# FFT convolution on Trainium2: blocks of 4 channels with both parts of the spectrum, in place of blocks of 8 channels of one part

## The chip, the core and the metric

The kernel runs on one core of one Trainium2 chip. A core has five engines with instruction streams of their own: TensorE (PE in the profile; its weight loads stand apart as PEld), VectorE (DVE), ScalarE (ACT), GpSimd (POOL) and SyncE (SP), which here does nothing but issue DMAs. They work on an on-chip memory of 128 partitions; TensorE writes to a second one, PSUM, from which VectorE and ScalarE copy. The metric is the device time of one launch in microseconds (us).

## The reference, cut to what matters

The input is a sequence of 2048 rows of 512 channels in bf16. Two kinds of layer alternate, each on a layer norm of its input, each added to it:

```python
x = A_u
x = x + _A_ref(_layernorm(x), ...)     # long convolution
x = x + _B_ref(_layernorm(x), ...)     # local attention: 32 heads, 8 keys at distances 0, 2, ..., 14
x = x + _A_ref(_layernorm(x), ...)     # the same convolution, same parameters
x = x + _B_ref(_layernorm(x), ...)

def _A_ref(u, A_re, A_im, B_re, B_im, C_re, C_im, log_dt, Dskip):
    ...
    P = jnp.exp(logdA[:, :, None] * l[None, None, :])
    K = jnp.einsum("dn,dnl,dn->dl", Cc, P, dB).real        # a kernel of 2048 taps for each channel
    L2 = 2 * L
    Kp = jnp.pad(K, ((0, 0), (0, L)))
    ...
    Kf = rfft2(Kp[:, None, :])
    Uf = rfft2(up[:, :, None, :])
    Yf = Uf * Kf[None, :, :, :]
    y = irfft2(Yf, (1, L2))[:, :, 0, :L]
    return y + u * Dskip
```

What the change touches is the convolution: the spectrum of the input times the kernel's spectrum, a complex product for each channel and frequency, and the way back. Both convolution layers have the same kernel, so its spectra are worked out in the first and kept in device memory for the second.

## The kernel before, in words

**Stages.** The program runs a short preparation, the first convolution together with the making of the kernel spectra (`kernel_and_first_conv`, to about 206 us), the first attention layer (`b_layer`), the second convolution (`a_layer`, about 323 to 377 us) and the second attention layer. X, the running sum, stays on chip throughout.

**The transform.** A row index is 16p + j, with p over the 128 partitions and j from 0 to 15. The transform of a channel is made in two stages.
- First stage (L840 in the first convolution, L1119 in the second): for each j, two matmuls (real and imaginary part) of 128 channels, into `ps_s`. Copies take it to `Z` (L845, L1123), which holds [128 frequencies k1, 16 groups of 8 channels, 2 parts, 16 j x 8 channels].
- Turn: a block is 4 groups, that is 32 channels with both parts, 128 x 1024 values in 8 squares of 128 x 128. It is transposed into `zt` either by one DMA on SP's queue (L854, L1134) or by 8 matmuls against the identity and a copy (`pt`, L871 and L1140, copies at L1144). Each square holds one part of 8 channels, so that its 128 partitions are 16 j x 8 channels. There are four blocks for each of four groups of 128 channels.
- Second stage (`mm2` L860 to L863, `s2` L1158 to L1161): 4 matmuls of 512 columns against the constants `C2` (cosine, sine and minus sine, each spread over 8 channels by a Kronecker product): real part from real and imaginary, imaginary part from both. The result `xp` is copied to `sp_u` or `xc` for the input (L867, L1165) and to `sp_k` for the kernel.

**The product.** Spectrum x = (xr, xi) times kernel k = (kr, ki). Two products of 1024 on VectorE (L931 and L932, L1176 and L1177): pa = (xr kr, xi kr), pb = (xr ki, xi ki), the kernel part repeated over both halves. Then, in some blocks, two half-sized additions on VectorE (the join: L936 and L937, L1181 and L1182) make the complex product, and the inverse's second stage takes 8 matmuls of 256 columns against `IC`; in the other blocks there is no join, and the inverse takes 16 such matmuls, which add the four partial products in PSUM (L951 to L955, L1196 to L1200). Which blocks are joined is part of the written order.

**The way back.** `vp` is copied to `VT` in two halves (L959, L1205); when the four blocks of a channel group are done, `final` multiplies by `F1T`, adds X with a matmul against the identity (`ps_y`, L978 and L981, L1219 and L1222), and a copy writes X (L985, L1227).

**The kernel spectra.** In the first convolution tables of exponentials are built on VectorE (`Ttab`, `Y2tab`, L391 and L456; some sums go through TensorE instead, `ps_sum` L431 and L432, with a copy on ScalarE, L436), contracted on TensorE (`psk` L469 and L472), stored and fetched again in another layout (`k_scratch`), and transformed as above. Each block of `sp_k` is stored to `kt_scratch` (L922, 256 KB, 16 in all). The second convolution loads it into `Kt` (L1235, one DMA of 256 KB for a block, four tiles of four blocks), issued on SP's queue as soon as the space that `Kt` takes is free; it lies over tiles of the first attention layer.

**The order of the work.** Nothing is scheduled at run time or by the compiler. Five lists of numbers (`ORDERS`), one for each stage, say in which order the operations are issued; the operations are registered with `pl.op`, and where there are alternatives (`pl.either`: a turn by DMA or TensorE, a copy on ScalarE or VectorE, a join or none, a sum on VectorE or on TensorE and ScalarE) the list holds the one that is taken. Each engine issues its own part of the list in that order and waits, at each instruction, for what it needs. Tiles come from pools of a fixed number of buffers (`sp_k` 4, `sp_u` 8, `zt` 4 and 6, `xc` 4, `pa` and `pb` 2 and 3).

Two places that the steps of the prediction rest on:

```python
nc.vector.tensor_tensor(pa[:], x[:], k[:, 0:1, :].to_broadcast([128, 2, 512]), ALU.mult)
nc.vector.tensor_tensor(pb[:], x[:], k[:, 1:2, :].to_broadcast([128, 2, 512]), ALU.mult)
...
Kl[dc, c] = pl.op("S", 0.35, lambda dc=dc, c=c: nc.sync.dma_start(Kt[dc][:, c], kt_dram[dc, :, c]), lag=2.0)
```

Of the kernel before, what the change touches and what calls it, by code (L numbers as in the profile page):

```python
# [11 lines left out]
ALU = mybir.AluOpType  # L12
# [32 lines left out]
STASH = ()  # L45


# [3 lines left out]
def _fft_consts():  # L51
# [10 lines left out]
    cr = np.cos(a16)  # L62
    ci = -np.sin(a16)
    I8 = np.eye(8)

    def kron_jk(m):
        return np.einsum('jk,de->jdke', m, I8).reshape(128, 128)
    C2 = np.stack([kron_jk(cr), kron_jk(ci), kron_jk(-ci)], axis=1)
    crp = np.cos(a16).T
    cip = np.sin(a16).T  # L70

    def kron_kj(m):
        return np.einsum('kj,de->kdje', m, I8).reshape(128, 128)
    CR, CI = kron_kj(crp), kron_kj(cip)
    IC = np.stack([np.concatenate([CR, CI], axis=1), np.concatenate([-CR, -CI], axis=1),
                   np.concatenate([-CI, CR], axis=1)], axis=1)
# [46 lines left out]
def load_b_weights(nc, const, wqkv, wo):  # L123
# [9 lines left out]
    VX = const.tile([128, 2, NV + NJ, 256], BF, name="VX")  # L133
    nc.gpsimd.memset(VX[0:1, :, 0:NV], 0.0)
    return dict(wqk=wqk, wv=wv, wo=wo_t), VX

# [59 lines left out]
def load_params(nc, pp, prm):  # L196
# [16 lines left out]
    "1 2 5 3 7 8 9 10 24 25 11 229 12 15 13 29 30 14 33 26 34 21 27 20 233 44 50 41 297 46 51 47 22 61 58 56 68 23 59 "  # L213
    "60 37 69 74 72 237 42 86 75 235 48 87 38 88 100 231 90 298 299 300 245 91 303 77 76 239 253 101 104 108 249 225 "
    "241 106 93 304 107 115 307 92 136 120 247 122 251 109 227 255 123 137 114 308 152 156 154 243 158 320 321 155 258 "
    "159 256 259 257 125 166 164 260 174 261 168 167 311 301 175 322 302 185 323 190 169 262 191 312 324 263 180 270 "
    "305 184 182 325 306 183 264 268 266 206 326 196 317 198 131 139 200 207 309 138 292 201 327 294 290 199 219 288 "
    "146 310 213 212 218 328 124 280 276 313 314 315 141 147 130 286 282 284 316 272 140 278 274 318 296 319",
    "39 3 37 40 6 38 41 7 47 50 9 4 51 52 10 53 12 42 0 56 13 15 54 16 57 58 59 60 17 25 19 168 18 26 49 22 30 102 48 "
    "88 31 169 170 89 23 103 108 90 111 91 94 105 109 92 62 32 171 106 112 172 95 173 174 134 96 97 98 175 178 33 63 "  # L220
    "27 64 180 100 65 123 181 182 28 183 66 67 68 190 126 69 128 135 71 127 118 72 184 113 188 186 189 136 191 138 187 "
    "131 139 132 142 192 137 269 73 270 271 272 143 140 141 121 275 74 159 79 145 122 276 277 146 278 147 273 81 148 "
    "133 279 116 149 82 155 156 83 84 162 283 163 281 244 117 86 157 245 246 284 85 247 87 289 193 248 194 34 195 292 "
    "290 196 158 152 197 286 199 249 206 200 201 202 153 293 203 349 250 205 208 287 251 214 309 254 350 315 258 210 "
    "351 222 352 212 295 259 256 257 296 216 224 220 353 299 166 304 228 218 260 264 316 354 267 355 312 266 265 226 "
    "262 313 263 317 321 357 268 318 358 359 164 307 323 374 322 375 319 230 376 308 167 324 297 377 302 380 381 382 "
    "320 378 383 314 360 365 303 384 298 429 430 232 340 372 234 236 386 369 343 431 326 370 327 335 330 367 368 344 "
# [253 lines left out]
def prepare(nc, pp, pst, raw, identf, block, ones, M, cb, T, ln, X):  # L481
# [215 lines left out]
    pl.run()  # L697


def kernel_and_first_conv(nc, tc, C, prm, x2d, const, kt_dram, kscr, udram, eps):  # L700
    with ExitStack() as es:
        mt = es.enter_context(tc.tile_pool(name="k_mt", bufs=1))
        M = Multipliers(mt, const)
# [205 lines left out]
        def k_fft(dc):  # L909
# [8 lines left out]
            for c in range(n // 32):  # L918
                keep(dc, c)
# [810 lines left out]
```

## Time and profile before

| what | us |
|---|---|
| median of 3 runs | 496.88 |
| the 3 runs | 496.77, 496.88, 498.36 |
| span of the profiled execution (its own time), first to last instruction | 495.2 |

The median of the runs is 1.7 above the span of the profiled execution.

Busy time by stage, from the profile's view of stretches:

| stage | length | PE | VectorE | ScalarE | DMA share |
|---|---|---|---|---|---|
| preparation and first convolution, 0 to 206 | 206.0 | 145.3 | 195.7 | 172.3 | 0.54 |
| first attention layer, 206 to 322.8 | 116.8 | 108.0 | 106.1 | 72.1 | 0.30 |
| second convolution, 322.8 to 377.3 | 54.5 | 50.5 | 50.7 | 49.2 | 0.56 |
| second attention layer, 377.3 to 495.2 | 117.9 | 107.6 | 105.2 | 55.5 | 0.29 |

How to read the lines that follow. A group line names a line of the kernel, the engine, the operation, the tile written <- the tiles read, the shapes, and the number of instructions; after the bar stand the busy time in us and the mean length of one in ns, and after the second bar the idle time of that engine just before these instructions, and what ended it. A line of the timeline has the start, the length, and the instructions run together in it. A line of the stretches has the stretch, its length, and then the busy time of PE, PEld, VectorE, ScalarE and GpSimd, with the number of instructions, the granted clock of TensorE (1.00 is full), the share of time for which the DMA engines were busy, and GB/s. For SP, whose work is to issue DMAs, the same place holds its busy time alone. Successive instructions of an engine overlap by a little, so that the distance from start to start is shorter than the length.

### The profile page before, as it was taken

How to read it: one execution, taken by the hardware profiler on the slowest of the kernel's cores; microseconds unless marked ns; L12 is line 12 of the kernel's file. 1: busy time of each engine (PE TensorE's matmuls, PEld its weight loads, DVE VectorE, ACT ScalarE, POOL GpSimd, SP SyncE). 2: the span in 40 equal slices, each digit the busy share in tenths (PEclk: the TensorE clock that was granted, in tenths of full speed). 3: DMA queues.
4: the chain of work that ended last, by engine and by line, in shares of the span. 5: the costliest groups of instructions: out<-in, count | busy, mean ns of one | idle time of the engine just before them, and what ended most of it. 6: DMA issues, size and time to landing. Idle time of an engine off the chain costs nothing.

```text
span 495.2 us, 12551 instructions
## 1 busy us (share of the span) xinstructions
PE 411.3 (83%) x5262; PEld 244.4 (49%) x5279; DVE 457.7 (92%) x774; ACT 349.0 (70%) x522; POOL 13.0 (3%) x63
## 2 busy tenths in 40 slices
PE   2602397988898989789999889979998999997996
PEld 1501262665575667543355434565675434563343
DVE  6999999999999998859899999988999689999996
ACT  6999986988778769764664359878997657643340
POOL 0000000000000004000000000000000000000000
PEclk9999698999999999999999989989999999999999
DMA  8930025448556846280031232559901500222217
GB/s 263 197 160 0 1 68 130 81 115 192 114 114 162 152 109 195 68 126 32 18 91 38 58 65 42 165 125 210 182 4 21 112 29 31 77 61 58 42 29 205
DMA packets 101596, 48.81 MB, mean 99 GB/s; under 512 B 86443, under 2 KB 93868, under 8 KB 101284
## 3 DMA queue, kind: packets, MB, share of 16 engines
q1 hardware_dynamic: 101108, 47.62, 41.6%
q8 instruction: 41, 0.67, 0.6%
q10 hardware_dynamic: 432, 0.39, 0.2%
q14 instruction: 15, 0.12, 0.1%
HBM read 15.78 MB, written 8.13 MB: 48 GB/s over the span
## 4 chain that ended last, share of the span: by engine, by line
PE 35%; DVE 12%; DMA 8%; ACT 7%; issue 5%; SPq 1%; POOL 0%; DVEq 0%; ACTq 0%
PE ps_qk L1324 7%; PE po L1503 4%; DVE prod L1487 4%; PE ps_v L1344 4%; PE ps_o L1560 3%; DVE prod L1375 3%; DMA VX<-VX 2%; PE Lp L1385 2%; DMA zt<-Z 2%; PE ps_y L1222 1%; PE vp L1196 1%; PE vp L1200 1%; DMA xnT<-xn 1%; ACT L L1474 1%; ACT Z L845 1%
## 5 line engine op out<-in xcount | busy, mean ns | idle before, releaser
L1375 DVE TENSOR_TENSOR prod<-qT,kT 128x2048 bf16<-128x2048 bf16 (+1 forms) x80 | 76.9, 1006 | 12.6 <-ACT kT L1329 9.9
L1487 DVE TENSOR_TENSOR prod<-VX,L 128x2048 bf16<-128x2048 bf16 (+2 forms) x96 | 77.3, 862 | 1.3 <-DMA VX<-VX 1.0
L1324 PE MATMUL ps_qk<-xnT,wqk 128*128 128x512 bf16 x256 | 61.4, 380 | 1.5 <-DMA xnT<-xn 1.3
L1503 PE MATMUL po<-prod,sb_ident 128*128 128x512 bf16 x216 | 53.5, 379 | 4.8 <-DVE prod L1487 3.7
L1324 PEld LDWEIGHTS <-wqk 128*128 128x128 bf16 x256 | 22.8, 97 | 31.9 <-issue 9.7
L1503 PEld LDWEIGHTS <-sb_ident 128*128 128x128 bf16 x224 | 21.2, 98 | 31.3 <-DVE prod L1487 5.1
L1344 PE MATMUL ps_v<-wv,xnT 128*128 128x256 bf16 x256 | 32.1, 273 | 1.9 <-ACT xnT L1302 1.4
L431 PE MATMUL ps_sum<-Ttab,sb_ident 128*128 128x512 bf16 x36 | 15.1, 420 | 22.2 <-DVE Ttab L391 21.4
L1349 ACT CAST VX<-ps_v 128x512 bf16<-128x512 f32 x32 | 18.6, 587 | 19.8 <-PE ps_v L1344 19.7
L845 ACT CAST Z<-ps_s 128x1024 bf16<-128x1024 f32 (+1 forms) x32 | 29.4, 983 | 3.4 <-PE ps_s L840 2.4
L1560 PE MATMUL ps_o<-wo_t,oT 128*128 128x512 bf16 x108 | 29.4, 388 | 0.6 <-DVE X L1543 0.2
L1329 ACT CAST qT<-ps_qk 128x512 bf16<-128x512 f32 x31 | 17.9, 587 | 16.8 <-PE ps_qk L1324 16.7
L1344 PEld LDWEIGHTS <-xnT 128*128 128x128 bf16 x256 | 24.1, 98 | 10.0 <-issue 3.4
L1523 ACT CAST ot<-po 128x1024 bf16<-128x1024 f32 x14 | 13.8, 1014 | 21.4 <-PE po L1503 21.4
L1385 PE MATMUL Lp<-prod,sb_bones 128*32 128x512 bf16 x256 | 25.6, 390 | 3.6 <-DVE prod L1375 3.6
L456 DVE TENSOR_TENSOR Ttab<-Ttab,MPA 128x2048 bf16<-128x2048 bf16 (+2 forms) x20 | 28.4, 1434 | 0.1
L456 DVE TENSOR_TENSOR Y2tab<-Ttab,MPB 128x6144 bf16<-128x6144 bf16 (+1 forms) x13 | 27.3, 2123 | 0.6 <-PE psk L472 0.6
L1329 ACT CAST kT<-ps_qk 128x512 bf16<-128x512 f32 x32 | 18.7, 586 | 10.9 <-PE ps_qk L1324 10.7
L840 PEld LDWEIGHTS <-sb_F 128*128 128x128 bf16 x256 | 16.1, 103 | 18.3 <-issue 15.7
L153 DVE BATCH_NORM_STATS2 ln_st_b<-X 128x6 f32<-128x128 bf16 (+2 forms) x80 | 23.0, 358 | 0.3 <-ACT X L985 0.3
L436 ACT CAST Ttab<-ps_sum 128x1024 bf16<-128x1024 f32 (+1 forms) x20 | 18.3, 940 | 6.0 <-PE ps_sum L432 4.6
L469 PE MATMUL psk<-Ttab 128*32 128x64 bf16 x1024 | 21.5, 199 | 1.1 <-DVE Ttab L456 0.9
(228 smaller groups left out, 1035.2 us busy)
## 6 DMA issues: line engine op xcount, KB each, us to landing
X<-in_A_u_dram SPq DMA_DIRECT2D x8, 512.0 KB, 5.4
kt_scratch<-sp_k SPq DMA_DIRECT2D x16, 256.0 KB, 3.3
Kt<-kt_scratch SPq DMA_DIRECT2D x16, 256.0 KB, 5.0
k_scratch<-KTq SPq DMA_DIRECT2D x7, 256.0 KB, 2.6
KT<-k_scratch SPq DMA_DIRECT2D x7, 256.0 KB, 3.7
VX<-VX SPq DMA_DIRECT2D x4, 448.0 KB, 4.4
kT<-kT SPq DMA_DIRECT2D x8, 192.0 KB, 2.2
out_dram<-X SPq DMA_DIRECT2D x3, 512.0 KB, 3.6
```

The lines of the kernel that those rows point to most:

```text
L153: self.nc.vector.bn_stats(self.st[:, j, part, :], X[:, j, a:b])
L456: nc.vector.tensor_tensor(d, src.to_broadcast([128, c, n, 2 * EYB]), mm.to_broadcast([128, c * n, EYB, 2]), ALU.mult)
L469: nc.tensor.matmul(o.rearrange("e (s i) -> e s i", s=2), xs, T[:, 1:3, h, m // 2, :, t], start=(m == 0), stop=False, skip_group_check=True)
L845: nc.scalar.copy(box["Z", kind, dc][:, 0:n // 8, :, jq * 32:(jq + 1) * 32].rearrange("p g r k -> p r g k"), box.pop(("s1", kind, dc, jq))[ ...
L1324: nc.tensor.matmul(ps[:], wqk[:, ct, f0:f0 + 128], xnT[:, 4 * s:4 * s + 4, ct, :], start=(ct == 0), stop=(ct == 3))
L1329: copy((qT, kT)[which][fp][:, f2, o:o + 512], box.pop(("qk", which, fp, f2, s))[:])
L1344: nc.tensor.matmul(ps[:, jj].rearrange("p t h d -> p (t h d)"), xnT[:, j + jj, ct, :], wv[:, ct, fp * 256:(fp + 1) * 256], start=(ct == 0) ...
L1375: nc.vector.tensor_tensor(pr[:, 0:n2], qT[fp][:, a:a + n2, j0 * 128:j0 * 128 + 1024], kT[fp][:, a:a + n2, c0:c0 + 1024], ALU.mult)
L1385: nc.tensor.matmul(Lp[r0:r0 + 32, w // 4, :], bones[:, w % 4, :], pr[:, f2 - a, hb * 512:(hb + 1) * 512], start=(n == 1), stop=(n == 4), s ...
L1487: nc.vector.tensor_tensor(p2[:, 0:nj].rearrange("p j t d h -> p (j t) d h"), VX[:, fp, NV + a:NV + a + nj].rearrange("p j (t d h) -> p (j ...
L1503: nc.tensor.matmul(po[:, c:c + 512], ident[:], p2[:, k + j:k + j + 2].rearrange("p j t d h -> p (j t d h)"), start=(n == 1), stop=(n == W))
L1560: nc.tensor.matmul(ps, box["oT"][:, ft // 2, j, ft % 2, :], wo_t[:, ft, :], start=(ft == 0 and not res), stop=(ft == 3))
```

## The change

A block is now 8 groups of 4 channels, and a square of 128 x 128 holds both parts of 4 channels: 2 parts x 16 j x 4 channels on its partitions once it is turned. `Z` is [128, 32, 2, 64].
- The second stage multiplies by one constant of 128 x 128 that takes both parts to both parts: 2 matmuls of 512 columns for a block. Partitions 0 to 63 of the result are the real parts, 64 to 127 the imaginary parts.
- The kernel spectrum is held as [128, 2, 1024]: once as it is, and once with the two halves of the partitions swapped. In the first convolution the swapped copy is made either by two DMAs of 64 partitions on SP's queue (`trade`) or by two more matmuls against a constant with swapped columns and a copy (`again`). The new lists take `trade` for 15 of the 16 blocks. Only the unswapped copy is stored (256 KB as before), and the second convolution loads each block by three DMAs: the whole, and the two halves to the other half's partitions. `Kt` is now 16 tiles of 512 KB.
- The product is one instruction of 2048 for a block, the input's spectrum repeated: (xr, xi) times (kr, ki), and (xr, xi) times (ki, kr). There is no join.
- The inverse's second stage takes 16 matmuls of 128 columns for a block; the signs lie in `IC`.
- `sp_k` has 3 buffers (before 4), `sp_u` 7 (8). A route by which spectra of the input could be parked in device memory, which was not in use, is removed. VX, a tile of the attention layer, is taken and zeroed in each attention layer, before once for both.
- All five lists of the order are new, the attention layers' too, and in them some copies, sums and turns go another way than before (a copy on VectorE for one on ScalarE, and the like).

The core of the diff (the lists, the removed route and repeated passages left out):

```diff
-    C2 = np.stack([kron_jk(cr), kron_jk(ci), kron_jk(-ci)], axis=1)
...
+    I4 = np.eye(4)
+
+    def rows(m):
+        return np.einsum('rjsk,de->rjdske', m, I4).reshape(128, 2, 64)
+    fwd = np.stack([np.stack([cr, ci], axis=1), np.stack([-ci, cr], axis=1)], axis=0)
+    C2 = rows(fwd)
+    C2 = np.stack([C2.reshape(128, 128), C2[:, ::-1].reshape(128, 128)], axis=1)
+    c, z = np.cos(a16).T, np.sin(a16).T
+    re, im = np.stack([c, z], axis=1), np.stack([-z, c], axis=1)
+    IC = np.stack([rows(np.stack([re, -re], axis=0)).reshape(128, 128), rows(np.stack([im, im], axis=0)).reshape(128, 128)], axis=1)
...
-                    xp = box["xp", kind, dc, i] = psA.tile([128, 2, 512], F32, name="xp", tag="psA")
-                    nc.tensor.matmul(xp[:, 0, :], C2[:, 0, :], z[:, :, 0, :], start=True, stop=False)
-                    nc.tensor.matmul(xp[:, 0, :], C2[:, 2, :], z[:, :, 1, :], start=False, stop=True)
-                    nc.tensor.matmul(xp[:, 1, :], C2[:, 1, :], z[:, :, 0, :], start=True, stop=False)
-                    nc.tensor.matmul(xp[:, 1, :], C2[:, 0, :], z[:, :, 1, :], start=False, stop=True)
...
+        def second(kind, dc, i, after, copies):
+            z, swap = ("zt", kind, dc, i), ("swap", dc, i)
+
+            def mm(k):
+                zt = box.pop(z) if k or kind == "u" or (swap, 0) in pl.taken else box[z]
+                xp = box["xp", kind, dc, i, k] = psA.tile([128, 1024], F32, name="xp", tag="psA")
+                for h in range(2):
+                    nc.tensor.matmul(xp[:, h * 512:h * 512 + 512], C2[:, k, :], zt[:, h * 4:h * 4 + 4, :], start=True, stop=True)
...
+            def trade():
+                x = box[kind, dc, i]
+                nc.sync.dma_start(x[0:64, 1, :], x[64:128, 0, :])
+                nc.sync.dma_start(x[64:128, 1, :], x[0:64, 0, :])
...
+                Pd["ks", dc, i] = pl.either(swap, lambda: pl.op("S", 0.9, trade, a, lag=2.4), lambda: again("A", 0.92, nc.scalar.copy),
+                                            lambda: again("V", 1.14, nc.vector.tensor_copy))
+                Sd["k", dc, i] = pl.op("S", 0.35, lambda: nc.sync.dma_start(kt_dram[dc, :, i], box["k", dc, i][:, 0, :]), a,
+                                       drop=("kt", dc, i), lag=3.0)
...
-                nc.vector.tensor_tensor(pa[:], x[:], k[:, 0:1, :].to_broadcast([128, 2, 512]), ALU.mult)
-                nc.vector.tensor_tensor(pb[:], x[:], k[:, 1:2, :].to_broadcast([128, 2, 512]), ALU.mult)
...
-                nc.vector.tensor_tensor(pa[:, 0, :], pa[:, 0, :], pb[:, 1, :], ALU.subtract)
-                nc.vector.tensor_tensor(pa[:, 1, :], pa[:, 1, :], pb[:, 0, :], ALU.add)
...
+                pp = box["pa", dc, c] = wk.tile([128, 2, 1024], BF, name="pa", tag="pa")
+                nc.vector.tensor_tensor(pp[:], x[:].unsqueeze(1).to_broadcast([128, 2, 1024]), k[:], ALU.mult)
...
+                for g in range(8):
+                    for k in range(2):
+                        nc.tensor.matmul(vp[:, g // 4, :, g % 4, :], pp[:, k, g * 128:(g + 1) * 128], IC[:, k, :],
+                                         start=(k == 0), stop=(k == 1))
...
-                Kl[dc, c] = pl.op("S", 0.35, lambda dc=dc, c=c: nc.sync.dma_start(Kt[dc][:, c], kt_dram[dc, :, c]), lag=2.0)
+                def load(dc=dc, c=c):
+                    t = Kt[dc][c]
+                    nc.sync.dma_start(t[:, 0, :], kt_dram[dc, :, c])
+                    nc.sync.dma_start(t[0:64, 1, :], kt_dram[dc, 64:128, c])
+                    nc.sync.dma_start(t[64:128, 1, :], kt_dram[dc, 0:64, c])
+                Kl[dc, c] = pl.op("S", 1.2, load, lag=3.0)
```

## The prediction

> **What bounds the kernel now.** I read the per-core view first (one core, mean granted clock 0.979, so no throttle to explain), then busy time by stretches, then the chain that ended last, then the groups of the lines that change, then the timeline of the DMA queue.
>
> ```profile
> core 0: us, PE busy (x) PEld busy (x) DVE busy (x) ACT busy (x) POOL busy (x), PEclk, DMA share, GB/s
> 70.00:110.00 40.00, 33.67 (x889) 20.32 (x887) 39.38 (x47) 32.64 (x39) 0.71 (x6) 0.96 0.46 101
> 110.00:150.00 40.00, 36.37 (x770) 24.79 (x768) 39.76 (x49) 32.50 (x42) 0.47 (x4) 1.00 0.70 148
> 150.00:200.00 50.00, 44.69 (x933) 32.54 (x932) 47.33 (x81) 40.44 (x58) 6.06 (x1) 1.00 0.66 158
> ...
> 335.00:345.00 10.00, 9.68 (x73) 6.05 (x73) 8.76 (x18) 9.72 (x13) 0.00 (x0) 1.00 1.03 215
> 345.00:355.00 10.00, 9.68 (x83) 6.74 (x83) 9.61 (x20) 8.50 (x14) 0.00 (x0) 1.00 0.94 188
> 355.00:365.00 10.00, 10.00 (x85) 7.14 (x84) 9.83 (x20) 10.00 (x19) 0.00 (x0) 1.00 0.38 76
> ```
>
> Two stages are touched. In the first (tables, kernel spectra and first convolution, up to about 206 us) VectorE is busy for 98 to 99% from 70 to 150 us: the bound is VectorE's sum of work. In the second convolution layer (first matmul at 322.85, last copy of X from 376.70) TensorE, VectorE and ScalarE are all near full, and up to 355 the DMA engines are too.
>
> ```profile
> PE 35%; DVE 12%; DMA 8%; ACT 7%; issue 5%; SPq 1%; POOL 0%; DVEq 0%; ACTq 0%
> ```
>
> The chain changes engine all the time; no single wait carries the end. So I sum the work of each engine by stage, and then look for new waits.
>
> ```profile
> L1176 DVE TENSOR_TENSOR pa<-xc,Kt 128x1024 bf16<-128x1024 bf16 x16 | 11.0, 686 | 0.7 <-ACT xc L1165 0.5 <-ACT X L1227 0.2
> L1181 DVE TENSOR_TENSOR pa<-pa,pb 128x512 bf16<-128x512 bf16 x15 | 6.3, 420 | 0.2
> L936 DVE TENSOR_TENSOR pa<-pa,pb 128x512 bf16<-128x512 bf16 x6 | 2.5, 420 | 0.1
> L1375 DVE TENSOR_TENSOR prod<-qT,kT 128x2048 bf16<-128x2048 bf16 x48 | 56.6, 1218 | 1.7 <-ACT qT L1329 0.6 <-ACT kT L1329 0.6 <-DMA kT<-kT 0.5
> ```
>
> ```profile
> 337.98 0.42 DVE L1181 TENSOR_TENSOR pa<-pa,pb 128x512 bf16<-128x512 bf16 x1
> 338.07 0.27 PE L1196 MATMUL vp<-sb_IC,pa 128*128 128x256 bf16 x1
> 338.18 0.27 PE L1200 MATMUL vp<-sb_IC,pa 128*128 128x256 bf16 x1
> 338.32 0.42 DVE L1182 TENSOR_TENSOR pa<-pa,pb 128x512 bf16<-128x512 bf16 x1
> 371.43 0.61 PE L1222 MATMUL ps_y<-VT,sb_F1T 128*128 128x128 bf16 x8
> ```
>
> Durations overlap, so I price by start to start: a join half 0.34 (337.98 to 338.32), a 1024-wide product 0.60, a 2048-wide one 1.14 (its step on the chain, 1.218 long). A 256-column matmul takes 0.109 in a stream, a 512-column one 0.2135, and one of 128 columns with its own weights 0.056: eight take 0.61, of which the last one's own length is 0.22.
>
> **The change part by part.** Counts are from the two programs' instruction orders, laid beside each other.
>
> First stage, VectorE. Joins: 12 halves go, -4.1. Products: 16 pairs of 0.60 become 16 single ones of 1.14, -1.0. Four table sums (three of 0.61, one of 1.14) go to TensorE and ScalarE, -3.0. The new order gives it more copies: three VT (0.61), one X of 1024 (1.15), four multiplier copies and one norm (0.33), +4.6. Net -3.5. TensorE: 62 matmuls of 512 fewer in the second stage (-13.2), the inverse 22.7 to 14.3 (208 of 0.109 become 256 of 0.056), 20 more for sums (+4.3): -17. ScalarE: some 5.6 more for table sums, some 2.4 less for multipliers; at 81% it covers that, and if that cover is gone it costs 3. With VectorE as the bound the stage gives -3.5 before new waits.
>
> The new wait there: 15 of 16 kernel blocks get their swapped half by two 64-partition DMAs on SP's queue, and the product waits for them. Price: two issues (0.32 to 0.57 by the stores and loads) and a landing of 2.1 to 3.7 (the copies kT<-kT), some 3.4. In the new order 11 blocks have 2.3 to 11 us of VectorE work between swap and product, which hides it. Four have 0.08, 0.68, 0.76 and 0.95. Behind a waiting product stand VectorE's last table pieces, and TensorE's contraction waits for those. Ends: 0, if their ScalarE feeds are late anyway, and 11 (4 x 3.4 - 2.5). They lie late in the stage; from 183 to 190 VectorE was busy 5.81 of 7.00, so there is slack, and I take 2. First stage: -1.5. The swaps also stand ahead of transposes on SP's queue; it issues there for under 40% of the time, so I price that at nothing; without that slack it would be some 10 us of issues.
>
> Second convolution layer. VectorE: 30 join halves -10.2, products -1.0, four more xc copies (1.15) +4.6, two more X copies +1.2, Z copies +0.1, two norms fewer -0.7: -6.0. TensorE: 32 matmuls of 512 fewer -6.8, inverse 14.8 to 14.3, one more block turned +0.45: -6.9. ScalarE: four xc fewer -4.2, two X -1.2, Z -0.2, one zt more +1.0: -4.6. The least, ScalarE's 4.6, is what the layer can give while all three are full.
>
> The inverse's 0.056 is the uncertain price: the new output runs are 4 values, before 8. Ends 0.056 and 0.109 (the row of twice the columns); I take 0.056, the row of the same columns. [...] The 2048-wide product, too, has its broadcast on the other operand: ends 1.14 and 2.29 (twice, as the 4096-wide row); 1.14 is the row of the same size.
>
> Now SP and the DMA engines:
>
> ```profile
> 304.75 7.31 SPq L1528 DMA_TRANSPOSE oT<-ot  x3
> 314.11 6.23 SPq L1235 DMA_DIRECT2D Kt<-kt_scratch  x10
> 328.75 7.63 SPq L1134 DMA_TRANSPOSE zt<-Z  x5
> 336.42 0.58 SPq L1235 DMA_DIRECT2D Kt<-kt_scratch  x1
> ...
> 320.00:322.00 2.00, 1.00 1.02 352
> 322.00:324.00 2.00, 1.00 0.98 370
> ```
>
> Ten loads of 256 KB took 6.23 to issue (0.62 each) and ran at about 360 GB/s. The new order puts 12 loads ahead of the first transpose, each now three DMAs and 512 KB. Their start still waits for the last oT transposes, about 314. Call the price of one such load c: at least 1.45 (512 KB at 352 to 370 GB/s), at most by the issues 1.86 (3 x 0.62). The first transpose then goes at 331.4 to 336.3 instead of 328.75. Fourteen transposes take 1.5 each (330 to 350 held 11 of them and five loads of 0.75 on full DMA engines), two loads lie between, and from the last transpose's data to the layer's end lie some 11 us (landing 2.5, second stage 0.6, copy 1.05, product 1.14, inverse 1.1, two VT 1.2, four output groups 2.64, last copy 0.6). End: 314 + 12c + 21 + 2c + 11 = 366 to 372. It was 377.3, less 4.6 is 372.7: the DMAs stay just behind the compute. Two of the first four blocks are turned on TensorE, which bridges the late first transpose. The layer gives -4.5. [...]
>
> Attention layers: the order gives VectorE 1.2 more in the first and 4.3 more in the second (casts, additions to X), ScalarE about as much less. The casts fall where VectorE had 8.17 busy of 12.00 (384 to 396); ends -1 and +4, I take +0.5. VX moves into the layer; its zeroing (6.06 on POOL) is off the chain: 0.
>
> Sum: -1.5 - 4.5 + 0.5 = -5.5 on the profiled span of 495.2. The median of the runs, 496.88, is 1.7 above that span, which I take as unchanged: 491.4.
>
> **The rivals.**
> A, slower: the loads clog the queue. One mechanism, the price c of a block's three DMAs. From 346 + 14c the layer is longer than before for c over 2.24; at c = 2.5 it ends at 381, +3.7, total 499.6. For it: the DMA share of 0.94 to 1.03 up to 355, and no 64-partition load in this trace. Against it: 352 to 370 GB/s.
> B: the swaps stall VectorE by 5 to 8 in the first stage: 494.5 to 497.5. For it: the four short distances. Against: VectorE has free time late in that stage.
> C: no new wait costs anything and VectorE's sums count in full: -3.5 - 6.0, total 487.4.
> D, slower: 128-column matmuls with runs of 4 run at 0.109: +13.6 on the layer's TensorE, net +6.7, total 502. Against it: runs of 8 run at the full column rate.
> That the change does nothing is excluded: the instructions are gone.
>
> **How the numbers follow.** A difference of 0.3% (1.5 us) is about what a measurement of this kernel can tell. Forecast 0.50 (488.5 to 494), C 0.16, B 0.13 (half of it still faster, the rest split), A 0.15, D 0.06. Faster 0.50 + 0.16 + 0.06 = 0.72, less a little for orders that I cannot price in the attention layers: 0.70; same 0.06; slower 0.24. The range reaches from 485.5 (C with the attention layers' -1 and a little more) to 500 (A at c = 2.5); beyond it lie D, the worse half of A and little below.
>
> **What would show it.** No L936 or L1181 groups; products of 1.22 in single rows, not 2.3; xp matmuls half as many; vp matmuls 0.056 apart. VectorE's idle time before the sp_k products under 3 us in all, named after the DMA sp_k<-sp_k. Stage ends: near 204.5 for the first, and the second convolution layer about 4.5 shorter. The first zt transpose of that layer 17 to 22 us after the first Kt load. Wrong if vp steps exceed 0.08, if the Kt loads take over 27 us before that transpose, or if the attention layers move by more than 3.

## The result, and the profile after

The changed kernel takes 533.96 us (median of 4 runs, 531.72 to 539.47) against 496.82 for the kernel before (median of 4, 495.28 to 498.36). The ratio is 1.0762, with a 95% interval of 1.0701 to 1.0823: it is 7.6% slower, where 1.1% faster was forecast, and outside the range. The profiled execution has a span of 537.7, and its own time is 539.47, the slowest of the four; the stages below add up to that span. The other three executions had spans of 529.9 to 532.8, so the differences below are together some 5 to 8 larger than in those.

| stage | before | after | difference | predicted |
|---|---|---|---|---|
| preparation and first convolution | 204.97 | 231.29 | +26.3 | -1.5 |
| first attention layer | 117.88 | 121.36 | +3.5 | +0.5 for both |
| second convolution | 54.49 | 63.08 | +8.6 | -4.5 |
| second attention layer | 117.88 | 121.95 | +4.1 | |
| span | 495.2 | 537.7 | +42.5 | -5.5 |

The first and third stage end where TensorE starts the `idle` matmuls of the next one, the second ends at the first matmul `ps_s<-U`.

First the sums, since the prediction was built from them. Over the whole run VectorE was busy 453.5 (before 457.7, so -4.2; the prediction's three stages add up to -3.5 - 6.0 + 5.5 = -4.0, with the attention layers' 1.2 and 4.3), TensorE 405.7 (411.3) and ScalarE 342.5 (349.0). No group of joins is left. These are the groups of the changed lines:

```profile
L933 DVE TENSOR_TENSOR pa<-sp_u,sp_k 128x2048 bf16<-128x2048 bf16 x16 | 19.3, 1217 | 6.0 <-DMA sp_k<-sp_k 5.7 <-PE vp L946 0.3
L1145 DVE TENSOR_TENSOR pa<-xc,Kt 128x2048 bf16<-128x2048 bf16 x16 | 19.0, 1218 | 2.4 <-ACT X L1183 2.2 <-ACT xc L1136 0.2
L1157 PE MATMUL vp<-sb_IC,pa 128*128 128x128 bf16 x256 | 16.3, 219 | 3.1 <-DVE VT L1163 1.8 <-DVE pa L1145 0.5 <-ACT xc L1136 0.3
```

So over the run the work went down by about what was forecast, and the time went up. (By stage the sum fits less well: in the first VectorE's fell by 5.9, 195.0 to 189.1, where 3.5 was forecast.) The time is in idling, as the stretches of the first stage show (columns as before: length, PE, PEld, VectorE, ScalarE, GpSimd, granted clock, DMA share, GB/s):

```profile
0.00:231.00 231.00, 140.10 (x3355) 102.62 (x3373) 189.14 (x277) 173.33 (x238) 3.22 (x23) 0.89 0.55 130
70.00:110.00 40.00, 26.17 (x643) 16.78 (x646) 36.32 (x43) 26.68 (x31) 0.56 (x4) 0.83 0.40 85
110.00:150.00 40.00, 27.88 (x668) 19.66 (x672) 28.77 (x29) 27.09 (x35) 0.51 (x4) 0.83 0.58 128
```

VectorE was busy 39.38 and 39.76 of 40 in the same two stretches before; now it is 36.32 and 28.77. In the whole stage it idles for 231 - 189 = 42, where before it idled for some 10 (206.0 - 195.7). The chain that ended last has DMA at 11% and issue at 10%, before 8% and 5%:

```profile
PE 39%; ACT 20%; DVE 15%; DMA 11%; issue 10%; SPq 4%; another core or an unknown queue 1%; ACTq 0%; DVEq 0%
```

The waits of VectorE between 30 and 232 (total, number, longest) name what it idles for:

```profile
DVE Y2tab L450 <- PE psk L466: 12.3, 2, 8.0
DVE pa L933 <- DMA sp_k<-sp_k: 5.7, 3, 2.8
DVE Ttab L361 <- PE psk L466: 5.2, 4, 2.2
DVE Ttab L385 <- ACT Ttab L430: 3.8, 2, 2.0
DVE X L974 <- PE ps_y L970: 3.0, 1, 3.0
```

Before, the waits for `psk` came to 0.6 and none of the other four stood in the list. 17.5 of it is now for `psk`: the contraction of the tables on TensorE, which must be done before VectorE may write the next table over the old one. And TensorE, which makes `psk`, waits itself (0 to 232):

```profile
...
PE psk L463 <- issue: 8.2, 4, 2.6
PE ps_s L833 <- DMA KT<-k_scratch: 5.7, 2, 5.1
PE psk L463 <- DVE Ttab L450: 5.4, 3, 3.6
PE ps_s L833 <- ACT Ttab L430: 5.2, 3, 4.6
...
PE psk L466 <- issue: 3.8, 2, 2.5
```

"issue" is time in which the engine waited for nothing that the profile shows. (Three rows left out above, 21.8, 8.8 and 6.9, are waits in the first 60 us; the kernel before has them too, with 21.4, 11.8 and 1.6.) Of the five shown, the fourth stood before with 8.4; the waits for `KT` and for `Ttab` from VectorE were 0.4 and 0.9, and there were no issue waits of `psk`. The loss does not sit in one place. The large product that fills `Y2tab`, one for each eighth of the channels, started before at 52.0, 65.3, 83.1, 94.5, 116.0, 130.9, 153.7 and 170.4, and now at 51.7, 66.0, 89.0, 103.2, 127.3, 147.7, 175.5 and 192.9: the seven steps lost 1.1, 5.2, 2.8, 2.5, 5.5, 5.1 and 0.6. 8.7 of it was lost by 103.2, when no swap had been issued yet (the first one goes at 106.76).

In the second convolution the queue of SP shows the loads ahead of the transposes (start, length, what):

```profile
344.24 0.34 SPq L1193 DMA_DIRECT2D Kt<-kt_scratch  x1
344.64 1.38 SPq L1194 DMA_DIRECT2D Kt<-kt_scratch  x1
346.06 0.58 SPq L1195 DMA_DIRECT2D Kt<-kt_scratch  x1
...
368.94 0.44 SPq L1195 DMA_DIRECT2D Kt<-kt_scratch  x1
369.90 11.16 SPq L1108 DMA_TRANSPOSE zt<-Z  x7
```

and TensorE standing for the first of these:

```profile
375.21 1.03 PE L1132 MATMUL xp<-zt,sb_C 128*128 128x512 bf16 x2 [11.05 <-DMA zt<-Z]
...
378.84 1.06 PE L1157 MATMUL vp<-sb_IC,pa 128*128 128x128 bf16 x16
```

The 36 DMAs of 12 blocks took 369.90 - 344.24 = 25.7 before the first transpose could go, and TensorE waited 11.05, although two blocks had been turned on TensorE ahead of them.

### The profile page after: what moved, and what is told of

Read it like the earlier page. It is cut to its first block, busy times and chain, and to the rows that moved or that the text cites. A ratio compares the mean times of both kernels' runs of the same rounds, so it can differ in the third digit from the quotient of the medians.

```text
span 537.7 us, 12783 instructions
## 1 busy us (share of the span) xinstructions
PE 405.7 (75%) x5333; PEld 248.2 (46%) x5370; DVE 453.5 (84%) x722; ACT 342.5 (64%) x509; POOL 19.3 (4%) x64
## 4 chain that ended last, share of the span: by engine, by line
PE 39%; ACT 20%; DVE 15%; DMA 11%; issue 10%; SPq 4%; another core or an unknown queue 1%; ACTq 0%; DVEq 0%
PE ps_qk L1288 9%; DMA Kt<-kt_scratch 4%; DVE prod L1451 4%; DVE prod L1339 3%; PE po L1467 3%; PE ps_v L1308 3%; PE ps_o L1524 3%; PE psk L463 2%; PE ps_s L833 2%; PE Lp L1349 2%; ACT X L663 2%; ACT Z L838 2%; PE psk L466 2%; DMA zt<-Z 2%; PE vp L946 2%
## 5 line engine op out<-in xcount | busy, mean ns | idle before, releaser
L425 PE MATMUL ps_sum<-Ttab,sb_ident 128*128 128x512 bf16 x46 | 19.4, 421 | 24.7 <-DVE Ttab L385 21.8
L463 PE MATMUL psk<-Ttab 128*32 128x64 bf16 x1024 | 23.7, 208 | 14.3 <-issue 8.2
L463 PEld LDWEIGHTS <-Ttab 128*32 128x32 bf16 x1024 | 21.1, 106 | 19.4 <-issue 19.2
L833 PEld LDWEIGHTS <-sb_F 128*128 128x128 bf16 x256 | 20.2, 120 | 21.3 <-issue 14.1
L466 PE MATMUL psk<-Y2tab,Ttab 128*32 128x48 bf16 x1024 | 23.5, 203 | 3.8 <-issue 3.8
L430 ACT CAST Ttab<-ps_sum 128x1024 bf16<-128x1024 f32 (+1 forms) x28 | 23.5, 887 | 3.4 <-PE ps_sum L426 3.2
```

The costliest lines, as they stand in the source:

```text
L463: nc.tensor.matmul(o.rearrange("e (s i) -> e s i", s=2), xs, T[:, 1:3, h, m // 2, :, t], start=(m == 0), stop=False, skip_group_check=True)
L466: nc.tensor.matmul(o[:, EYB:].rearrange("e (q i) -> e q i", q=3), xs, Y2[:, :, h, 1 - m // 2, :, t], start=False, stop=(m == 3), skip_grou ...
L833: nc.tensor.matmul(o, F1[:, j, r, :], rhs(j), start=True, stop=not dk)
```

## The experiments

Thirteen kernels were compared with the kernel before. Stage lengths are those of one profiled execution each. The changed kernel and four of these have the same first convolution, and there it took 227.8 to 231.3, mean 229.1: differences of less than about 2 in that stage say nothing. In the same way the second convolution took 60.8 to 63.4, mean 62.5, in the five kernels that have the changed kernel's list and loads for it and its list for the layer before, and the two attention layers together 240.3 to 243.3, mean 241.6, in the eight that have its lists for them.

### Swaps, loads, and the attention layers' orders, one at a time

`no_swap` leaves the two DMAs out:

```diff
             def trade():
-                x = box[kind, dc, i]
-                nc.sync.dma_start(x[0:64, 1, :], x[64:128, 0, :])
-                nc.sync.dma_start(x[64:128, 1, :], x[0:64, 0, :])
+                pass
...
-  x[:].unsqueeze(1).to_broadcast([128, 2, 1024]), k[:], ALU.mult)
+  x[:].unsqueeze(1).to_broadcast([128, 2, 1024]), k[:, 0:1].to_broadcast([128, 2, 1024]), ALU.mult)
```

> The changed kernel without the swap DMAs of the first convolution; the product reads the unswapped spectrum for both halves, so the spectra's product is not the right one. The first convolution (start to the idle matmuls ahead of the first attention layer) is 231.3 us in the changed kernel, 205.0 before. Theory S, the swaps are the cause (VectorE waits 5.7 us for them directly, and transposes and loads stand behind them on SP's queue): 205 to 212, total near 512. Theory O, the new order on TensorE is the cause (the contraction's 512 instructions stand in a row, and TensorE has gaps of 2 to 3 us in it that no event of the profile explains, 14 us in all): 222 to 228, total 525 to 531, and the gaps before psk stay.

Measured: first convolution 223.87; in all 531.29, ratio 1.0663 (1.0643 to 1.0684). Against the mean of 229.1 the swaps cost 5.2, against the profiled execution of the changed kernel 7.4. That is the price of rival B, and a fifth to a good quarter of the stage's loss.

`kt_whole` leaves out the two half loads in the second convolution, and the product reads the first half twice. `kt_two` puts one 256 KB load over all 128 partitions in their place, so that the bytes are the same:

```diff
                     nc.sync.dma_start(t[:, 0, :], kt_dram[dc, :, c])
-                    nc.sync.dma_start(t[0:64, 1, :], kt_dram[dc, 64:128, c])
-                    nc.sync.dma_start(t[64:128, 1, :], kt_dram[dc, 0:64, c])
+                    nc.sync.dma_start(t[:, 1, :], kt_dram[dc, :, c])          # kt_two only
```

> The changed kernel with only the 256 KB load for each block in the second convolution; the two 64-partition loads are left out, and the product reads the unswapped half twice. The second convolution took 63.1 us (352.65 to 415.74), before 54. If the 32 half loads are the cause, the first zt transpose comes 8 to 10 us after the first load, not 25.7, the 11 us wait of TensorE for zt goes, and the layer takes 49 to 53: total 12 less, near 522. If the layer is slow for its order or its matmuls, it stays over 58.

> The changed kernel with the swapped half replaced by a second load of the whole 128 partitions (same bytes, two DMAs of 256 KB for a block in place of one of 256 and two of 128 KB); the second half is not swapped. If the bytes are the price, 512 KB at the 350 to 370 GB/s of 256 KB loads is 1.45 us a block: the twelve blocks take 17 to 18 us and the layer 56 to 58. If the price is in the 64-partition halves alone, the same; if it is in the DMA engines whatever the shape, 2.1 us a block and 63 as now.

Measured: second convolution 49.78 and 57.30, after 63.08; in all 521.62, ratio 1.0487 (1.0454 to 1.0520), and 528.61, ratio 1.0619 (1.0572 to 1.0665). The queue of SP in `kt_whole`:

```profile
341.05 7.75 SPq L1193 DMA_DIRECT2D Kt<-kt_scratch  x12
355.83 11.20 SPq L1108 DMA_TRANSPOSE zt<-Z  x7
```

Twelve whole blocks take 7.75 to issue, 0.65 each, and the queue then stands idle from 348.80 to 355.83, when the first transpose goes. The three forms of one load cost 0.65 (256 KB), 1.55 (512 KB over 128 partitions, 338.92 to 357.5) and 2.14 (512 KB, half of it over 64 partitions). So of the 13.3 between 49.78 and 63.08, the second half, as one more load of 256 KB over 128 partitions, makes 7.5, and having it moved by two DMAs over 64 partitions, in place of one over 128, another 5.8. That is two changes in one, the third DMA and the 64 partitions: in the changed kernel the second to the fifth block take 1.75 each, with the three DMAs issued one right after the other, the later ones 2.0 to 2.95. No run separates the two. Without either the layer is 4.7 shorter than before (54.49 to 49.78): the arithmetic's gain, forecast at 4.6, is there.

`b_orders` puts before's lists for the two attention layers back:

```diff
-ORDERS[2], ORDERS[4] of the changed kernel
+ORDERS[2], ORDERS[4] of the kernel before
```

> The changed kernel with the two attention layers in the order of the kernel before. They took 121.35 and 121.96 us, before 117.9 and 118.2. If the new orders cost it (more copies on VectorE), they go back to 118 and 118.5, total 527. If it is the lower granted clock after a longer first convolution, or what the layers start with, they stay at 120 to 122.

Measured: attention layers 117.44 and 116.83, together 9.0 less than in the changed kernel's profiled execution (7.3 less than the mean of 241.6) and 1.5 less than before; in all 528.36, ratio 1.0595 (1.0555 to 1.0636). The second convolution took 65.06 here, longer than in any other run. The loss of the attention layers is in their new lists. Which of the moves in them makes it was not taken apart.

### The first convolution: its order with the old arithmetic

`new_order` is the kernel before, with its blocks, joins left out, its matmuls and its loads, issued in the changed kernel's order for the first convolution and the preparation:

```diff
 # kernel before
-ORDERS[0], ORDERS[1] of the kernel before
+ORDERS[0], ORDERS[1] of the changed kernel, swaps dropped, inverse with 16 matmuls
```

> The kernel before (blocks of 8 channels, no swaps, no half loads), with the preparation and the first convolution in the changed kernel's order; since that order has no joins, all 16 blocks of the first convolution go unjoined (16 matmuls of 256 columns each). The other stages are those of the kernel before. The first convolution takes 205.0 us in the kernel before, 224 in the changed kernel without swaps. If the order is what costs those 19 us, it takes 220 to 230 here too, and VectorE waits for psk again; if the blocks of 4 channels cost it, 204 to 209.

Measured: first convolution 234.09, the second 53.92, attention 115.84 and 116.60; in all 528.18, ratio 1.0575 (1.0509 to 1.0640). With no block, no constant and no swap of the change, the stage loses 29. "Order" here means the whole list: it also says on which engine an alternative runs (four table sums moved off VectorE, copies moved to it), and no run separates these choices from the places in the list. VectorE waited for `psk` here too, 10.5 and 5.5.

### Rows of contractions on TensorE

One thing that differs in the orders is how a contraction stands on TensorE. It is 256 small matmuls, each with a weight load of its own, in 8 pieces. The list before puts other matmuls between the pieces; the new list issues four contractions in unbroken rows of 512 instructions. `bunched` makes such rows of four contractions in the kernel before, `bunched_all` of seven; here the first:

```diff
 # kernel before, ORDERS[1]: pieces of contraction 1 are 88 to 92 and 94 to 96
-... 48 88 31 169 170 89 23 103 108 90 111 91 94 105 109 92 62 32 171 106 112 172 95 173 174 134 96 97 98 ...
+... 48 31 169 170 23 103 108 111 105 109 62 32 171 106 112 172 173 174 134 88 89 90 91 94 95 96 97 92 98 ...
```

> The kernel before with one thing moved: in four of the eight contractions of the first convolution (the same four as in the changed kernel) TensorE's 256 matmuls psk stand in a row, at the place where the last of them stood; before, other matmuls lie between them. If a row of short instructions starves TensorE (its next instructions come 2 to 3 us late), each of the four loses 1.5 to 4 us and VectorE waits for them: first convolution 211 to 220, total 503 to 512. If the order matters for other reasons, 205 to 207.

> The kernel before with seven of the eight contractions in unbroken rows (four gave 214.8 us for the first convolution, 205.0 without). If each row costs its own 2.4 us, 221 to 224; if the loss comes from two or three places where VectorE waits for the contraction anyway, 214 to 218.

Measured: first convolution 214.76 and 225.54, so +9.8 (2.4 for each row) and +20.6 (2.9 each); in all 508.45, ratio 1.0209 (1.0169 to 1.0249), and 516.94, ratio 1.0366 (1.0319 to 1.0413). The waits of TensorE, of `bunched` from 60 to 220:

```profile
PE psk L473 <- issue: 4.5, 2, 2.2
PE psk L476 <- issue: 4.3, 2, 2.3
```

and of `bunched_all` from 60 to 225:

```profile
PE psk L473 <- issue: 7.9, 4, 2.4
PE psk L476 <- issue: 5.7, 3, 2.3
```

There were no such waits in the kernel before, and now there are 8.8 and 13.6. But the edit also moves most pieces to a later place, and the waits are less than the loss; how much of it is the row and how much the delay was not separated.

`spread` goes the other way in the changed kernel, but not far: three groups of other matmuls are put between the pieces, two in the first of the four rows and one in the second; the other two rows stay unbroken. (The expectation counts six groups in all four rows; the list has three in two of them.)

```diff
 # changed kernel, ORDERS[1]
-... 88 89 90 91 23 94 95 62 190 96 92 24 97 102 98 63 111 ... 214 215 ... 265 298 304
+... 88 89 102 90 91 111 23 94 95 62 190 96 92 24 97 98 63 ... 214 298 215 ... 265 304
```

> The changed kernel with six matmul groups that followed the four unbroken contractions put between their pieces (two groups of the first stage in two of them, a second stage in each of the other two). If starving in the row costs time, these groups fill 0.45 us each of the gaps: first convolution 229 to 231 becomes 225 to 228. If not, no change (within 1).

Measured: first convolution 231.38; in all 535.81, ratio 1.0753 (1.0714 to 1.0791). Nothing gained. The issue waits of `psk` went from 12.0 to only 10.5: the longest in the two broken rows went from 1.4 to under 1 and from 2.2 to 1.4, those in the two unbroken rows stayed (2.6 and 2.5, now 2.9 and 2.4). VectorE waited for `psk` as long as ever:

```profile
DVE Y2tab L450 <- PE psk L466: 12.5, 2, 8.3
DVE Ttab L361 <- PE psk L466: 6.7, 4, 2.5
```

So making such rows in the kernel before cost this stage 2.4 each, but that they cost as much in the changed kernel is not shown.

### Loads of the tables' result, alone and without swaps

The longest wait of TensorE after the first 60 us of the stage is 5.1, from 128.2 on. It was for a `KT<-k_scratch` load that stood on SP's queue behind transposes: it was issued at 129.77 and landed by 133.28. `fetch_early` moves three such loads ahead; `no_swap_early` leaves the swaps out as well (as in `no_swap`).

```diff
 # changed kernel, ORDERS[1]: loads are 327, 328 and 525
-... 383 238 311 384 306 327 233 ... 34 316 328 329 ... 250 518 320 ... 508 525 506
+... 383 238 327 328 311 384 306 233 ... 34 316 329 ... 250 518 525 320 ... 508 506
```

> The changed kernel with three loads KT<-k_scratch of the first convolution put ahead of the transposes that stand before them on SP's queue. TensorE waited 5.1 and 1.2 us for two of them, and the contraction that VectorE waits 8 us for stands behind that wait. If this place in the queue is a part of the cost, the first convolution (228 to 231) takes 221 to 226; if the transposes that now come later cost the same, 228 to 231.

> The changed kernel without the swap DMAs (the product reads the unswapped spectrum for both halves) and with the three early loads of KT. If the two causes add, the first convolution takes 225.3 - 5.5, some 219 to 221, and what is left over the 205 of the kernel before, 14 to 16, is the order on TensorE and VectorE. If they were one cause (the swaps made the loads late), it takes 222 to 225.

Measured: first convolution 225.33 and 222.04; in all 532.41, ratio 1.0690 (1.0636 to 1.0745), and 526.69, ratio 1.0599 (1.0553 to 1.0645). Against the mean of 229.1 the places of the loads cost 3.8, loads and swaps together 7.1. The sum of the two prices taken alone, 9.0, is larger, but by no more than these single executions differ by, so whether they overlap is not shown. Without both of them the stage is still 17 longer than before.

### Other ways to fetch the second half

`kt_late` puts the loads of the second convolution in the order of their products, with 7 blocks ahead of the first transpose and 9 between. `both_halves` stores the swapped half too, in the first convolution, and loads a block by one DMA of 512 KB, 9 ahead; it has before's lists for the attention layers and the early loads.

```diff
 # kt_late: ORDERS[3]
-... 12 loads ahead of the first transpose
+... 7 loads ahead of the first transpose, 9 between, in the order of the products
 # both_halves
-  nc.sync.dma_start(kt_dram[dc, :, i], box["k", dc, i][:, 0, :])
+  nc.sync.dma_start(kt_dram[dc, :, i], box["k", dc, i][:])
...
-  nc.sync.dma_start(t[:, 0, :], kt_dram[dc, :, c])
-  nc.sync.dma_start(t[0:64, 1, :], kt_dram[dc, 64:128, c])
-  nc.sync.dma_start(t[64:128, 1, :], kt_dram[dc, 0:64, c])
+  nc.sync.dma_start(t[:], kt_dram[dc, :, c])
```

> The changed kernel with the loads of the second convolution in the order in which the products need them, 7 blocks ahead of the first transpose (12 before) and the other 9 between and after the transposes. The layer took 62 to 63 us. If the place of the loads ahead of the transposes is what costs, the first transpose goes near 15 us after the first load (25.7 before), and the layer takes 55 to 58; if the sum of all DMA work sets the end, the tail of the loads takes back the gain: 60 to 63.

> The changed kernel with four repairs: both halves of the kernel spectrum are stored in the first convolution (512 KB, after the swap), and the second loads them in one DMA of 512 KB over 128 partitions for a block, 9 ahead of the first transpose and 7 between; the attention layers in the order of the kernel before; the three early loads of KT. Second convolution: 12 blocks by two whole loads went at 1.55 us each, so first transpose 14 to 15 us after the first load, the sum of DMA work 16 x 1.5 + 21 and a tail of 11 end it at 50 to 53 (62 to 63 before). Attention 117 and 117. First convolution 222 to 230, for the swaps and the order of TensorE stay. Total 506 to 516, still slower than the kernel before: what is left is the first convolution's order.

Measured: `kt_late` 64.90 for the layer; in all 536.86, ratio 1.0788 (1.0741 to 1.0835). The first transpose goes 14.8 after the first load, not 25.7, and the layer is no shorter: it is not the place of the loads that costs, but their time together with that of the transposes. `both_halves` 55.60 for the layer, and 234.56 for the first convolution, against 225.33 with early loads alone; in all 527.21, ratio 1.0585 (1.0548 to 1.0622). The stores, twice as large and behind the swaps, cost in the first convolution what the plain load saves in the second, and more.

The queue of SP says the same in six traces. From the start of the first load's issue to the end of the last transpose's it takes 42.1 us in the kernel before, 51.6 in the changed one, 52.8 in `kt_late`, 45.7 in `kt_two`, 44.7 in `both_halves` and 37.9 in `kt_whole`. In all six the layer starts 8.4 to 8.7 after the first of these moments and ends 19.5 to 21.2 after the second, so that its length (54.5, 63.1, 64.9, 57.3, 55.6, 49.8) goes with the queue's time.

### The new arithmetic in the old order

If the order is the cause, the new blocks in the old order must be as fast as before. The changed kernel, which keeps swapped halves, has 3 buffers of `sp_k` and 7 of `sp_u`, before's lists were written for 4 and 8, and without the swapped halves there is room for these. So `old_order_free` is the changed kernel with no swap and whole loads only, `sp_k` 4 and `sp_u` 8, and before's lists throughout, the joins dropped.

```diff
-ORDERS of the changed kernel
+ORDERS of the kernel before, joins dropped
...
-  x = sp.tile([128, 1024], BF, name="sp_u", tag="sp_u", bufs=7)
+  x = sp.tile([128, 1024], BF, name="sp_u", tag="sp_u", bufs=8)
...
-  sp.tile([128, 2, 1024], BF, name="sp_k", tag="sp_k", bufs=3)
+  sp.tile([128, 1, 1024], BF, name="sp_k", tag="sp_k", bufs=4)
```

and the edits of `no_swap` and `kt_whole`.

> The blocks of 4 channels of the changed kernel in the order of the kernel before, in all stages; without joins, without the swap DMAs and with whole loads alone (the product reads the unswapped half for both, so the spectra's product is not the right one), and with the numbers of sp_k and sp_u buffers of the kernel before, for which there is room since no swapped half is kept. First convolution: the prediction's sums say that VectorE's work alone makes it some 3 us shorter than before; so 200 to 204 if the new order made the loss, and 215 to 225 if the blocks themselves (short matmuls, fewer long ones between the contractions) make it. Second convolution 49 to 52, attention 117 and 117. Total 484 to 490 in the first case, 500 to 508 in the second.

Measured: 494.99 (6 runs) against 498.26, ratio 0.9944 (0.9922 to 0.9966). Stages 202.75, 119.16, 53.44, 118.02. The first convolution is 2.2 shorter than before and 26.4 shorter than the mean of the changed kernel's. Its stretches and its waits of VectorE:

```profile
70.00:110.00 40.00, 28.60 (x865) 17.67 (x868) 39.38 (x45) 33.17 (x40) 0.72 (x6) 0.96 0.46 101
110.00:150.00 40.00, 30.07 (x750) 20.43 (x755) 39.76 (x45) 33.44 (x44) 0.48 (x4) 1.00 0.70 155
```

```profile
DVE pa L931 <- PE vp L944: 2.9, 1, 2.9
DVE pa L931 <- ACT sp_k L885: 2.3, 1, 2.3
DVE Y2tab L450 <- PE psk L466: 0.9, 1, 0.9
```

VectorE is busy 39.38 and 39.76 of 40 again, to the hundredth what it was before, and waits 0.9 for `psk` in place of 17.5. Old blocks in the new order 234.09, new blocks in the old order 202.75: the list makes the loss of this stage. (It isn't the number of buffers, which is before's in both.) Of the 26.4, some 7.1 are the swaps and the three late loads (`no_swap_early`); the other 19.3 are in the rest of the list, with whatever the fewer buffers add to it. Which of its moves make them was not taken apart.

TensorE's issue waits before `psk` are here too, 60 to 225:

```profile
PE psk L463 <- issue: 3.3, 4, 1.5
...
PE psk L466 <- issue: 1.7, 4, 0.7
```

They come to 5.0, none longer than 1.5, and VectorE waits only 0.9 for `psk`: such waits need not hold it up.

This run also says what the arithmetic is worth in before's order, with the swaps and the second halves for nothing: 0.56%. A list fitted to the new blocks might give more; none was run. No kernel here that does the whole work was faster than the kernel before.

## Why the prediction was wrong, point by point

**The sums of work: right over the run.** Products in single rows of 1.22 (1217 and 1218 ns), 16 inverse matmuls in 1.06, that is 0.056 apart ((1.06 - 0.22) / 15), VectorE 4.2 less. The double broadcast and the output runs of 4 cost nothing that shows (before, the 2048-wide `prod<-qT,kT` took 1218 ns and a 128-column matmul 0.056); rival D is out.

**First stage, -1.5: wrong, and it is most of the error.** The step that failed is "With VectorE as the bound the stage gives -3.5 before new waits". It took the bound for a property of the stage: VectorE at 98 to 99%, so the time is VectorE's sum. The bound was a property of the order, which had kept VectorE fed; with a new list it had to be shown again, for each `Y2tab` and each contraction. The prediction searched the new list for one new wait, the swaps, and priced all else by counts. In the new list VectorE idles 32 more than before. In before's lists only two of the terms apply, joins -4.1 and products -1.0 (the others are moves of the new list), and of these 5.1 the stage gave 2.2 (`old_order_free`): even there VectorE's sum did not come through in full.

**The swaps, 2 within 0 to 11: too low.** 5.2 to 7.4. Named right, with the wait on the right tile (5.7 in three waits), and rival B had its size. The slack late in the stage that was to hide them, 5.81 busy of 7.00 from 183 to 190, was slack of the old order.

**"that at nothing" for the swaps ahead of the transposes on SP's queue: wrong in part.** SP had time, but it issues in the order of its list: three loads behind waiting transposes cost some 3.8 (225.33 with them ahead, against the mean of 229.1), with a TensorE wait of 5.1 for one of them.

**Second convolution, -4.5: wrong in the term c and in the tail.** c was taken as 1.45 to 1.86 and measured 2.14, outside the range that the rows gave. The upper end was a price of issuing 128-partition DMAs; what the 64-partition ones take in the DMA engines was nowhere in the trace. What makes the 2.14 is not shown by the runs either, since a third DMA came with the 64 partitions (two DMAs over 128 partitions cost 1.55, `kt_two`). But even with 2.14 the formula would keep the layer shorter than before, since rival A's limit was 2.24. The other error is the 11 from the last transpose to the end. It was 415.74 - 395.8 = 20. The kernel before had it already, 377.34 - 356.18 = 21.2 by this line of its queue:

```profile
350.81 5.37 SPq L1134 DMA_TRANSPOSE zt<-Z  x4
```

The 11 was one block's way through the engines. In the changed kernel all three engines are nearly full in these 20 us (stretch 396 to 416, and the one ahead of it):

```profile
370.00:396.00 26.00, 18.24 (x209) 14.10 (x212) 14.55 (x15) 16.66 (x25) 0.00 (x0) 0.84 1.09 195
396.00:416.00 20.00, 18.11 (x253) 14.86 (x253) 18.49 (x35) 18.11 (x32) 6.07 (x1) 1.00 0.28 66
```

The last five transposes come 1.4 apart, while a block takes the engines 54 / 16 = 3.4: some five blocks are still to be done when the DMAs end, not one. That is not all of it: in `kt_late` the last transposes come 3.2 apart, the engines are 65 to 77% busy after them, and the end is 20.5 away all the same; why was not looked into. So the time of loads and transposes on SP's queue and these 20 us add up. "The DMAs stay just behind the compute" was the sentence that failed.

**The least of three engines, -4.6: met** where the second halves are not loaded (`kt_whole`, -4.7), though in the old order with whole loads it was only -1.05.

**Attention layers, +0.5: too low.** +7.6, by the mean of eight kernels +5.9; `b_orders` puts it on the new lists. The prediction said that it would be wrong if they moved by more than 3.

**The chances.** None of the five cases had the order itself in it. The text named "orders that I cannot price" for the attention layers alone and took 0.02 off for them. That an order of 532 operations is new was the largest unknown in this change, and it had no rival of its own.

## What to carry to other kernels

When a change comes with a new written order, the order is a change of its own: run the old arithmetic in the new order, or the new arithmetic in the old one, before pricing either. An engine at 99% is the bound only as long as every other engine delivers in time (VectorE from 110 to 150: 39.76 of 40 before, 28.77 in the new list), so in a forecast follow a few successive steps of it through the new list (here: table, contraction, next table), with the queue that each of their loads stands in. Where a layer's loads and transposes stand on one DMA queue, add up their times on it, wherever the loads stand among the transposes (63.1 and 64.9 here), and read the time from the last transpose to the layer's end from the profile of the kernel before.

## What the runs showed of the hardware that had not been expected

**Instruction supply on TensorE.** The profile has a queue for instructions; in the changed kernel (packets, MB, share):

```profile
q8 instruction: 42, 0.69, 0.5%
```

That is 42 packets of 16 KB beside TensorE's 5333 matmuls and 5370 weight loads, one for 255 of them (from 60 to 232, 23 packets beside 2974 and 2985, one for 259; in the kernel before 41 beside 5262 and 5279, one for 257). That the packets hold TensorE's instructions is read from these ratios. In rows of contractions, with eight matmuls in 0.07 to 0.09 us, TensorE stops for 1.9 to 2.6 us at about the time of such a packet: gaps at 99.7, 111.9, 159.4 and 186.9, packets at 99.2, 111.4, 159.4 and 187.2. In the whole run it has seven issue waits longer than 0.2, of 1.3 to 2.6, so most of the 42 packets come without such a gap; if the packets are the cause, the 8.8 of issue waits in the four rows of `bunched` are theirs. That the packet causes the gap is read from these times and was not tested by itself.

**64 partitions.** 512 KB cost 2.14 us with half of it moved by two 64-partition DMAs, and 1.55 in two DMAs over 128. The third DMA is a part of the difference that was not separated.

**The clock.** TensorE's granted clock was 0.83 from 70 to 150 us, where TensorE was busy 26.17 and 27.88 of 40. It was 0.96 and 1.00 in `old_order_free` with 28.60 and 30.07: nearly the same busy time, without the long gaps (between 70 and 150 the longest are 5.05 and 3.57 in the changed kernel, and none from 60 to 225 is over 2.0 in `old_order_free`). Whether the gaps make the lower clock was not tested, and what the lower clock itself cost was not separated. It is not needed for the loss: `new_order` was granted 0.96 and 0.91 in the same two stretches, and its first stage is 29.1 longer than before, that of the changed kernel 26.3.
